# Gated linear attention into two MLPs: the attention's stack in aligned rows, its chunk ends by a small matmul, its small copies on another engine

## Chip, cores and metric

The kernel runs on one core of one Trainium2 chip. The metric is the device time of one launch in microseconds (us), the median of several runs. Engines are TensorE (PE; PEld is its weight load), VectorE (DVE), ScalarE (ACT), GpSimd (POOL) and SyncE (SP, which here issues all DMAs).

## Reference, cut to what matters

```python
batch, n_heads, seq, head_dim = (4, 8, 768, 48)
mag = np.sqrt(a_re * a_re + a_im * a_im)
scale = np.minimum(mag, 0.999) / (mag + 1e-06)
a_re_n, a_im_n = (a_re * scale, a_im * scale)
...
for t in range(S):
    new_re = ar * S_re - ai * S_im
    new_im = ar * S_im + ai * S_re
    kv = np.einsum('bhd,bhe->bhde', k[:, :, t], v[:, :, t])
    S_re, S_im = (new_re + kv, new_im)
    y[:, :, t] = np.einsum('bhd,bhde->bhe', q[:, :, t], S_re)
...
x = y.transpose(0, 2, 1, 3).reshape(3072, 384)
h = x @ w_in;  g = np.maximum(0.01 * h, h);  x = g @ w_out            # first MLP, d_ff 2048
h = x @ w_in2; g = np.where(h > 0, h, np.exp(np.minimum(h, 0)) - 1)   # second MLP, d_ff 2048
out = g @ w_out2
```

The weights come as 64-bit floats.

## The kernel before, in words

**Attention.** The sequence is cut into 6 chunks of 128 steps; a chunk of one batch entry is a tile, 24 in all (tile i is chunk i // 4 of batch entry i % 4). In a tile the 384 feature rows (8 heads of 48) lie on 128 partitions in 3 groups j, as [128, 3, 128]. The front half of `attention` (up to `yield`, L409 to L452) loads the decay's real and imaginary part, makes its magnitude with Ln and Exp on ScalarE, its running product by a scan on VectorE (L438), the ratio of imaginary to real part (L431) and clamps it (L432), copies the product at the chunk's end to `flags` on GpSimd (L446), and multiplies k and q by the product or its inverse (L452). The back half takes the arctangent, sums the phase by a scan (L462), takes off whole turns by adding and subtracting a large constant (L466, L467, both VectorE), carries the end's phase to the next chunk by a small GpSimd operation (L471), and writes k and q times cosine and sine into `st` (L481). `st` has 257 columns a row: 128 of k, 128 of q, and the chunk-end product, which GpSimd copies there (L479).

Features have to come from "group and partition" to "head by head, cosine over sine", so `st` goes to DRAM (L488) and returns as `f` (L491), 96 rows by 8 heads by 257. The scores of each head are one matmul (L520), masked on VectorE (L525). In tiles 0 to 2 (`EARLY`) the output is 8 matmuls (L535), a ScalarE copy (L539) and 3 transposes on PE (L545); in later tiles it is made transposed (L558, with the carried state L563), copied to `am` by ScalarE (L568), sent to DRAM by two DMAs (L572) and fetched back by one (L575). From either, `split` makes the 16-bit high part `xh` (ScalarE, L368) and the rest `xl` (VectorE, L369), the input of the first MLP. The state is updated by 8 matmuls (L591) and, in odd chunks, multiplied by the chunk-end product, the last column of `f` (L603).

**MLPs.** Tokens are worked in 8 blocks of 384 (3 tiles). All matmuls of the MLPs take 16-bit high and low parts, three products for each: per block and per 128 of d_ff, 9 matmuls into `h` (L620), then ScalarE and VectorE make g and split it into `gh` and `gl` (L628 to L636), then 9 matmuls into `acc` (L655). Blocks of the first and second MLP alternate after two of the first (`ORDER`). Weights are loaded (L325, L328), turned into 32-bit floats on VectorE (L346, L348, L351) and split (L357 ScalarE, L358 VectorE), 32 times. Checks of the inputs' range run on ScalarE (L337, L339, L375, L380, L386) wherever there is room.

**Order.** Nothing is scheduled by the chip or the compiler: `Plan` takes every operation with an estimated duration, its dependences and a due time, lists them by rank, repeats that `ROUNDS` times backwards and forwards, and keeps the best. The operations are then issued in that order, so each engine's queue is fixed, and one that waits holds up everything behind it. Where the plan leaves TensorE idle for more than 0.7 us, dummy matmuls on `ident` are put in (L773), one for each 0.22 us of the planned gap, so that its clock stays up.

## Time and profile before

| | |
|---|---|
| three runs | 978.29, 980.07, 984.93 us; median 980.07 |
| the profiled execution | 977.53 us, of which the span from first to last instruction is 975.7 us |
| TensorE's granted clock over the span | 0.978 of full speed |
| busy | PE 926.8, DVE 681.6, ACT 700.2, POOL 52.3 us |
| DMA | 129.15 MB, 132 GB/s over the span |

The profile is of one execution. A line such as L620 is a line of the kernel before. In a timeline row the two numbers are start and duration in us, and the bracket gives the idle time of the engine before it and what ended it. 32-bit matmuls show as two entries each. Consecutive instructions of one engine overlap a little, so the distance of their starts is what each takes from the engine.

### The profile page before, as it was taken

The numbers are of one execution on the slowest core, as the hardware profiler recorded it, in microseconds if no ns is written. First come the engines' busy times: TensorE is split into PE (matmuls) and PEld (weight loads), VectorE is DVE, ScalarE is ACT, GpSimd is POOL, SyncE is SP. The second block draws the span as 40 slices with busy tenths as digits, with TensorE's granted clock in tenths as the row PEclk, the third lists the DMA queues.
The fourth block names the chain that finished last, engine by engine and source line by source line (L and its number), as shares of the span: only waits on it lengthen the run. The fifth ranks groups of instructions, "written<-read, shape, count | busy, mean of one in ns | idle before, by whom it ended". The sixth has DMA issues, their size and how long they took to land.

```text
span 975.7 us, 17221 instructions
## 1 busy us (share of the span) xinstructions
PE 926.8 (95%) x6444; PEld 616.9 (63%) x6444; DVE 681.6 (70%) x1322; ACT 700.2 (72%) x1526; POOL 52.3 (5%) x113
## 2 busy tenths in 40 slices
PE   3488999999999999999999999999999999999997
PEld 3487666676755666666766667666666666666664
DVE  7998999999984685655786458637886444445452
ACT  6676669576998899999998456539798544345552
POOL 3103001010000000000010000000000000000000
PEclk8698999999999999999999999999999999999999
DMA  7797793776747836955846004405446021000000
GB/s 249 202 260 208 207 238 106 201 226 190 212 146 205 235 102 186 247 150 171 239 137 153 17 19 119 116 1 131 120 149 171 1 57 50 17 1 1 23 3 28
DMA packets 110028, 129.15 MB, mean 132 GB/s; under 512 B 6768, under 2 KB 98672, under 8 KB 109936
## 3 DMA queue, kind: packets, MB, share of 16 engines
q1 hardware_dynamic: 109936, 127.97, 47.9%
q8 instruction: 52, 0.85, 0.4%
q14 instruction: 40, 0.33, 0.1%
HBM read 100.15 MB, written 27.80 MB: 131 GB/s over the span
## 4 chain that ended last, share of the span: by engine, by line
PE 49%; ACT 20%; DVE 15%; DMA 10%; issue 4%; POOL 1%; SPq 0%; DVEq 0%; ACTq 0%; POOLq 0%
PE h L620 22%; PE acc L655 22%; ACT wr L339 5%; DMA stack_scratch<-st 4%; DMA wr<-in_w_in 3%; ACT wt L337 2%; ACT gh L368 2%; PE pa L520 2%; DMA re<-in_aa 2%; DVE g L633 2%; DVE wt L348 2%; DVE gl L369 2%; DVE wr L351 1%; DVE st L481 1%; ACT g L631 1%
## 5 line engine op out<-in xcount | busy, mean ns | idle before, releaser
L620 PEld LDWEIGHTS <-w 128*128 128x128 f16 x2304 | 225.5, 98 | 151.0 <-issue 8.0
L369 DVE TENSOR_TENSOR gl<-g,gh 128x384 f16<-128x384 f32 x256 | 141.8, 554 | 91.7 <-ACT gh L368 89.9
L655 PE MATMUL acc<-gh,w 128*128 128x384 f16 x768 | 187.3, 326 | 0.9 <-ACT gh L368 0.8
L368 ACT ACTIVATE gh<-g 128x384 f16<-128x384 f32 x256 | 132.6, 518 | 76.6 <-DVE g L633 73.6
L655 PE MATMUL acc<-w,gh 128*128 128x384 f16 x768 | 187.4, 326 | 0.0
L633 DVE SCALAR_TENSOR_TENSOR g<-h,g 128x384 f32<-128x384 f32 x256 | 141.6, 554 | 62.4 <-ACT g L628 59.1
L655 PEld LDWEIGHTS <-w 128*128 128x128 f16 x1152 | 112.6, 98 | 75.7 <-issue 2.5
L620 PE MATMUL h<-xh,w 128*128 128x384 f16 x768 | 146.6, 327 | 2.7 <-DVE g L633 2.7
L620 PE MATMUL h<-yh,w 128*128 128x384 f16 x768 | 146.8, 328 | 1.1 <-DVE g L633 1.1
L655 PE MATMUL acc<-gl,w 128*128 128x384 f16 x384 | 125.2, 326 | 0.2
L655 PE MATMUL acc<-w,gl 128*128 128x384 f16 x384 | 125.2, 326 | 0.1
L655 PEld LDWEIGHTS <-gh 128*128 128x128 f16 x768 | 74.5, 98 | 48.3 <-issue 0.9
L628 ACT ACTIVATE g<-h 128x384 f32<-128x384 f32 x128 | 61.8, 483 | 55.5 <-PE h L620 55.2
L630 ACT ACTIVATE g<-h 128x384 f32<-128x384 f32 x128 | 62.1, 485 | 48.2 <-PE h L620 45.9
L632 DVE TENSOR_SCALAR g<-g 128x384 f32<-128x384 f32 x128 | 45.6, 357 | 72.6 <-ACT g L631 72.4
L620 PE MATMUL h<-yl,w 128*128 128x384 f16 x384 | 83.4, 326 | 0.0
L620 PE MATMUL h<-xl,w 128*128 128x384 f16 x384 | 83.3, 326 | 0.0
L631 ACT ACTIVATE g<-g 128x384 f32<-128x384 f32 x128 | 66.1, 518 | 1.9
L339 ACT ACTIVATE wr<-wt,consts 128x768 f32<-128x768 f32 x64 | 64.1, 1002 | 0.4
L655 PEld LDWEIGHTS <-gl 128*128 128x128 f16 x384 | 37.6, 98 | 25.3 <-DVE gl L369 0.5
L520 PE MATMUL pa<-f 96*128 96x128 f32 x384 | 48.4, 276 | 4.4 <-DMA f<-stack_scratch 2.2
L520 PEld LDWEIGHTS pa<-f 96*128 96x128 f32 x384 | 46.6, 192 | 6.7 <-issue 3.2
(104 smaller groups left out, 1173.9 us busy)
## 6 DMA issues: line engine op xcount, KB each, us to landing
wr<-in_w_out SPq DMA_DIRECT2D x64, 384.0 KB, 3.9
wr<-in_w_in SPq DMA_DIRECT2D x64, 384.0 KB, 4.4
stack_scratch<-st SPq DMA_DIRECT2D x48, 385.5 KB, 5.0
f<-stack_scratch SPq DMA_DIRECT2D x48, 385.5 KB, 5.9
kq<-in_kq SPq DMA_DIRECT2D x24, 384.0 KB, 5.3
...
```

The lines of the kernel that those rows point to most:

```text
L337: plan.op("ACT", act(2 * DM), lambda: S_.activation(t.t, raw.t[:, :, :, 1].bitcast(F32), AF.Abs), r=both, w=[t])
L339: plan.op("ACT", act(2 * DM) + 2 * EXTRA, lambda side=side, scale=scale, bias=bias: S_.activation(raw.t[:, :, :, 0].bitcast(F32), t.t, AF. ...
L368: plan.op("ACT", eng, lambda: S_.activation(hi(), v(), AF.Copy), r=r, w=wh)
L369: plan.op("DVE", dve(n), lambda: V.tensor_tensor(lo(), v(), hi(), ALU.subtract), r=r + wh, w=wl)
L520: T_.matmul(pt.t[:, hh * C:(hh + 1) * C], lhsT=f.t[:, h, 0:C], rhs=f.t[:, h, C:2 * C], start=True, stop=True)
L620: T_.matmul(ph.t[:, :n], lhsT=w.t[:, 0, z, j * P:(j + 1) * P], rhs=x.t[:, j, :n], start=(m == 0), stop=(m == len(seq) - 1))
L628: plan.op("ACT", act(n, True), lambda: S_.activation(g.t[:, :n], ph.t[:, :n], AF.Copy, scale=0.01 * c), r=[ph], w=[g])
L630: plan.op("ACT", act(n, True), lambda: S_.activation(g.t[:, :n], ph.t[:, :n], AF.Relu, scale=-1.0 / (SX * SW)), r=[ph], w=[g])
L631: plan.op("ACT", act(n), lambda: S_.activation(g.t[:, :n], g.t[:, :n], AF.Exp, scale=-1.0), w=[g], table="L")
L632: plan.op("DVE", dve(n, True), lambda: V.tensor_scalar(g.t[:, :n], g.t[:, :n], -1.0, SG, ALU.add, ALU.mult), w=[g])
L633: plan.op("DVE", dve(n), lambda: V.scalar_tensor_tensor(g.t[:, :n], ph.t[:, :n], c, g.t[:, :n], ALU.mult, ALU.max), r=[ph], w=[g])
L655: T_.matmul(acc[o].t[:, :width], lhsT=pair[0], rhs=pair[1], start=(f == 0 and m == 0), stop=(f == KF - 1 and m == 2))
```

## The change

- Features are laid out another way: partition 16h + e, group j holds feature 3e + j of head h. So one partition's three rows of `st` are neighbours in DRAM, and a store is one run of 3072 bytes for each partition. The 257th column is gone: rows are 1024 bytes. The host lays out the inputs so; rows of `w_in` are permuted on the host (`X_ROWS`).
- The chunk-end product reaches the state by a matmul: in odd chunks VectorE spreads the three end values over 96 columns (`rows`), one matmul with a 0/1 matrix gives [96, 8] in PSUM, and the state is multiplied by that.
- The copies to `flags` and the carry run on VectorE; the two copies into `st` are gone. GpSimd has no work left in the loop.
- The clamp ahead of the arctangent is gone. The addition of the large constant to the phase runs on ScalarE.
- All tiles make the output transposed. `xh` and `xl` are made from PSUM directly; each has a fourth group that holds heads 6 and 7, and four small DMAs (16 partitions x 3 x 128 16-bit values, from `xh` into `xh` and from `xl` into `xl`) spread it over the partitions that the heads of 48 rows leave free. The DRAM round trip of the output and the transposes of the early tiles are gone.
- The plan's costs of the stack's DMAs are lower, its rounds 11 instead of 3. So the order of instructions is another one throughout.

```diff
-    ROUNDS = 3
+    ROUNDS = 11
...
+    nc.vector.tensor_reduce(row_of, ident.rearrange("p (h e) -> p e h", h=H), AX.X, ALU.add)
+    nc.vector.tensor_reduce(head_of, ident.rearrange("p (h e) -> p h e", h=H), AX.X, ALU.add)
...
-        plan.op("DVE", dve(N, True), lambda: V.tensor_scalar(w.t, w.t, -TAN_MAX * RC, TAN_MAX * RC, ALU.max, ALU.min),
-                w=[w])
...
-        plan.op("POOL", 200, lambda: G.tensor_copy(flags.t[:, 3:6, i], pr.t[:, :, 1, C - 1]), r=[pr], w=[f3])
+        plan.op("DVE", dve(KJ), lambda: V.tensor_copy(flags.t[:, 3:6, i], pr.t[:, :, 1, C - 1]), r=[pr], w=[f3])
...
-        plan.op("DVE", dve(N, True), lambda: V.tensor_scalar(nf.t, ph.t, MAGIC, None, ALU.add), r=[ph], w=[nf])
+        plan.op("ACT", act(N), lambda: S_.activation(nf.t, ph.t, AF.Copy, bias=MAGIC), r=[ph], w=[nf])
...
-            plan.op("POOL", 200, lambda: G.tensor_scalar(cr.t, nf.t[:, :, C - 1], -1.0, None, ALU.mult), r=[nf], w=[cr])
+            plan.op("DVE", dve(KJ), lambda: V.tensor_scalar(cr.t, nf.t[:, :, C - 1], -1.0, None, ALU.mult), r=[nf], w=[cr])
...
-        st = plan.buf(cp, [P, 2, KJ, CW], F32, "st", ST_BUFS)
+        st = plan.buf(cp, [P, 2, KJ, 2 * C], F32, "st", ST_BUFS)
-            plan.op("POOL", 200, lambda cs=cs: G.tensor_copy(st.t[:, cs, :, 2 * C], flags.t[:, 3:6, i]),
-                    r=[f3], w=[st.part(("e", cs))])
...
-            plan.op("SP", 1800, lambda cs=cs: nc.sync.dma_start(
-                scr[cs].rearrange("(j p) w -> p j w", p=P), st.t[:, cs]),
-                r=[st.part(("e", cs)), st.part(cs)], w=[dr.part(cs)])
-            plan.op("SP", 2350, lambda cs=cs: nc.sync.dma_start(
+            plan.op("SP", 1150, lambda cs=cs: nc.sync.dma_start(
+                scr[cs].rearrange("(p j) w -> p j w", j=KJ), st.t[:, cs]), r=[st.part(cs)], w=[dr.part(cs)])
+            plan.op("SP", 1900, lambda cs=cs: nc.sync.dma_start(
                 f.t[D * cs:D * (cs + 1)], scr[cs].rearrange("(h d) w -> d h w", d=D)), r=[dr.part(cs)], w=[f.part(cs)])
...
-                    kn.t[:, :, cs, :], pt.t[:, :DM].rearrange("p (h d) -> p h d", h=H), AF.Copy),
+                    kn.t[:, :, cs], pt.t[:, :DM].rearrange("p (j h e) -> p h e j", j=KJ, h=H), AF.Copy),
...
-        if i < EARLY:
...
-            plan.op("ACT", act(512, True), lambda: S_.activation(
-                yt.t[:wide].rearrange("p g t -> p (g t)"), py.t[:wide], AF.Copy, scale=SX), r=[py], w=[yt])
-            yd, ys = yt_dram[i % 2], plan.buf(None, None, None, "yscr", 2)
-            for r in range(2):
-                plan.op("SP", 290, lambda r=r: nc.sync.dma_start(
-                    yd.rearrange("(g r e) t -> r e g t", r=2, e=D)[r], yt.t[64 * r:64 * r + D]), r=[yt], w=[ys.part(r)])
-            y = plan.buf(cp, [P, KJ, C], F32, "y")
-            plan.op("SP", 1000, lambda: nc.sync.dma_start(y.t, yd.rearrange("(j p) t -> p j t", p=P)),
-                    r=[ys.part(0), ys.part(1)], w=[y])
...
-        split(lambda: xh.t[:, :, cut], lambda: xl.t[:, :, cut], xap, act(N, i < EARLY), N, [xsrc], [xh.part(q)],
-              [xl.part(q)])
+        py4 = lambda: py.t[:wide].rearrange("p (g t) -> p g t", g=4)
+        plan.op("ACT", act(512, True), lambda: S_.activation(xh.t[:wide, :, span], py4(), AF.Copy, scale=SX), r=[py], w=[xh])
+        plan.op("DVE", dve(512), lambda: V.scalar_tensor_tensor(
+            xl.t[:wide, :, span], py4(), SX, xh.t[:wide, :, span], ALU.mult, ALU.subtract), r=[py, xh], w=[xl])
+        for z, xz in enumerate((xh, xl)):
+            for r in range(2):
+                plan.op("SP", 200, lambda xz=xz, r=r: nc.sync.dma_start(
+                    xz.t[64 * r + D:64 * (r + 1), 0:KJ, span],
+                    xz.t[64 * r:64 * r + D, KJ, span]),
+                    r=[xz], w=[x1[k][z].part((q, r))])
...
             if c % 2:
-                plan.op("DVE", dve(N), lambda: V.tensor_tensor(state[b].t, state[b].t, pe(), ALU.mult),
-                        r=fp, w=[state[b]])
+                rows = plan.buf(cp, [P, 2, DE, KJ], F32, "rows")
+                plan.op("DVE", 120, lambda: V.tensor_tensor(
+                    rows.t, flags.t[:, 3:6, i].unsqueeze(1).unsqueeze(1).to_broadcast([P, 2, DE, KJ]),
+                    row_of.unsqueeze(1).unsqueeze(3).to_broadcast([P, 2, DE, KJ]), ALU.mult), r=[f3], w=[rows])
+                pe = pa()
+                plan.op("PE", 100, lambda: T_.matmul(
+                    pe.t[:2 * D, :H], lhsT=rows.t.rearrange("p a e j -> p (a e j)"), rhs=head_of, start=True, stop=True),
+                    r=[rows], w=[pe])
+                plan.op("DVE", dve(N), lambda: V.tensor_tensor(
+                    state[b].t, state[b].t, pe.t[:2 * D, :H].unsqueeze(2).to_broadcast([2 * D, H, D]), ALU.mult),
+                    r=[pe], w=[state[b]])
```

**Order on TensorE**, from the scores of tile 2 (L520 before, L510 in the change) to the first matmuls of the first MLP (L620, now L596). `pa` is a PSUM buffer of the attention, `h` the hidden layer's; L773, now L750, are the dummy matmuls. Before:

```order
L520 MATMUL pa<-f 128x128 x8
L773 MATMUL h<-ident 128x128 x6
L535 MATMUL pa<-v,am 128x48 x8
L773 MATMUL h<-ident 128x128 x2
L545 MATMUL pa<-ident,y 128x128 x3
L591 MATMUL pa<-v,kn 96x48 x8
L507 MATMUL pa<-ident,st 128x128 x3
L620 LDWEIGHTS w_143
L620 MATMUL h<-xh,w_143 128x384
```

In the change, the end of the same stretch (the output matmuls L530 come in four such pairs):

```order
L530 MATMUL pa<-am,v 64x128
L530 MATMUL pa<-am,v 48x128
L559 MATMUL pa<-v,kn 96x48 x8
L750 MATMUL h<-ident 128x128 x18
L596 LDWEIGHTS w_146
L596 MATMUL h<-xh,w_146 128x384
```

The transposes of y and those of tile 3's `st` are no longer ahead of the first MLP matmul; 18 dummy matmuls are.

**Order on VectorE** in the same stretch, from the first masking of tile 2 to its `xl`. `wt`, `wr` and `w` are a weight's stages, `t_` buffers are the attention's temporaries. Before:

```order
L525 TENSOR_TENSOR am<-pa,mask 128x512
L466 TENSOR_SCALAR t_765<-t_752 128x384
L525 TENSOR_TENSOR am<-pa,mask 128x512
L467 SCALAR_TENSOR_TENSOR t_765<-t_765,t_752 128x384
L346 TENSOR_SCALAR wt<-wr 128x768
L358 SCALAR_TENSOR_TENSOR w_750<-wr,w_750 128x2x384
L348 SCALAR_TENSOR_TENSOR wt<-wr,wt 128x768
L481 TENSOR_TENSOR st<-kq,t_790 128x3x256
L481 TENSOR_TENSOR st<-kq,t_765 128x3x256
L369 TENSOR_TENSOR xl<-pa,xh 128x3x128
```

In the change:

```order
L515 TENSOR_TENSOR am<-pa,mask 128x512
L432 SCALAR_TENSOR_TENSOR pr<-t_691,flags,consts 128x128 x3
L515 TENSOR_TENSOR am<-pa,mask 128x512
L347 TENSOR_SCALAR wt<-wr 128x768
L427 TENSOR_TENSOR t_736<-im,t_613 128x384
L349 SCALAR_TENSOR_TENSOR wt<-wr,wt 128x768
L440 COPY flags<-pr 128x3
L571 TENSOR_TENSOR rows<-flags,row_of 128x96
L352 SCALAR_TENSOR_TENSOR wr<-wr,wt 128x768
L544 SCALAR_TENSOR_TENSOR xl<-pa,xh 112x4x128
```

Tile 3's phase and its `st` stood between tile 2's masking and its `xl`; they have moved behind it, and work of a front half stands there.

**Order on SyncE's queue** from the stores of tile 0's stack to the loads of tile 1's. Before:

```order
L488 DMA stack_scratch<-st 128x3x257 x2
L451 DMA kq<-in_kq 128x768
L491 DMA f<-stack_scratch 48x8x257 x2
L328 DMA wr<-in_w_out 128x768
L325 DMA wr<-in_w_in 128x3x256
L488 DMA stack_scratch<-st 128x3x257 x2
L451 DMA kq<-in_kq 128x768
L328 DMA wr<-in_w_out 128x768
L325 DMA wr<-in_w_in 128x3x256
L491 DMA f<-stack_scratch 48x8x257
```

In the change:

```order
L480 DMA stack_scratch<-st 128x768 x2
L445 DMA kq<-in_kq 128x768
L482 DMA f<-stack_scratch 48x8x256 x2
L480 DMA stack_scratch<-st 128x768 x2
L445 DMA kq<-in_kq 128x768
L329 DMA wr<-in_w_out 128x768
L326 DMA wr<-in_w_in 128x3x256
L482 DMA f<-stack_scratch 48x8x256 x2
```

One pair of weight loads that stood ahead of tile 1's stores has moved away.

## Rows read from the trace of the kernel before

**Rows 1.** The page: PE and DVE busy in 40 slices (tenths).
```profile
PE   3488999999999999999999999999999999999997
DVE  7998999999984685655786458637886444445452
```

**Rows 2.** Stretches: length, busy PE, PEld, DVE, ACT, POOL; PE clock, DMA share, GB/s.
```profile
60.00:80.00 20.00, 17.79 (x160) 17.21 (x159) 19.01 (x38) 14.77 (x30) 4.56 (x4) 1.00 0.92 251
...
88.40:960.00 871.60, 862.14 (x5952) 557.37 (x5950) 600.87 (x1178) 638.72 (x1409) 31.63 (x74) 1.00 0.46 124
...
320.00:340.00 20.00, 18.09 (x137) 13.05 (x137) 13.40 (x28) 17.33 (x41) 1.25 (x4) 0.91 0.92 242
```

**Rows 3.** Timeline, 80 to 91 us, POOL, ACT, PE and DVE in turn.
```profile
80.51 3.08 POOL L471 TENSOR_SCALAR carry<-t 128x3 f32<-128x3 f32 x1 [2.77 <-DVE t L467]
...
83.62 0.52 ACT L476 ACTIVATE t<-t 128x384 f32<-128x384 f32 x1 [1.99 <-POOL carry L471]
...
84.57 0.90 PE L545 MATMUL pa<-ident,y 128*128 128x128 f32 x3 [2.84 <-ACT y L539]
85.27 2.69 PE L591 MATMUL pa<-v,kn 128*96 128x48 f32 x16
...
88.42 2.07 PE L620 MATMUL h<-xh,w 128*128 128x384 f16 x6
...
90.81 1.14 PE L620 MATMUL h<-xh,w 128*128 128x384 f16 x6
...
84.17 0.96 DVE L481 TENSOR_TENSOR st<-kq,t 128x768 f32<-128x768 f32 x1 [0.67 <-ACT t L476]
86.04 0.56 DVE L369 TENSOR_TENSOR xl<-pa,xh 128x384 f16<-128x384 f32 x1 [0.90 <-ACT xh L368]
```

**Rows 4.** Timeline of VectorE, 20 to 31 us.
```profile
20.81 0.55 DVE L448 TENSOR_TENSOR t<-pr,t 128x384 f32<-128x384 f32 x1
21.28 0.95 DVE L348 SCALAR_TENSOR_TENSOR wt<-wr,wt 128x768 int32<-128x768 int32 x1
22.15 0.55 DVE L449 SCALAR_TENSOR_TENSOR pr<-t,t 128x384 f32<-128x384 f32 x1
...
29.95 1.24 DVE L462 TENSOR_TENSOR_SCAN t<-t,consts 128x128 f32<-128x128 f32 x3
```

**Rows 5.** Groups: busy us, mean ns of one, idle before.
```profile
L525 DVE TENSOR_TENSOR am<-pa,mask 128x512 f32<-128x512 f32 x48 | 32.6, 683 | 7.3 <-PE pa L520 4.3 <-DMA turned_scratch<-am 3.1
...
L466 DVE TENSOR_SCALAR t<-t 128x384 f32<-128x384 f32 x24 | 8.5, 353 | 0.2
...
L746 DVE COPY ok<-subn 128x1 f32<-128x1 f32 x1 | 0.1, 146 | 0.0
...
L755 PE MATMUL pa<-consts,okr 128*1 128x1 f32 x2 | 0.2, 164 | 0.0
```

**Rows 6.** DMA issues: KB each, median us from issue to landing.
```profile
stack_scratch<-st SPq DMA_DIRECT2D x48, 385.5 KB, 5.0
f<-stack_scratch SPq DMA_DIRECT2D x48, 385.5 KB, 5.9
...
turned_scratch<-am SPq DMA_DIRECT2D x42, 96.0 KB, 2.6
```

**Rows 7.** Timeline of TensorE, 54 to 62 us.
```profile
54.77 1.48 PE L591 MATMUL pa<-v,kn 128*96 128x48 f32 x16
56.09 1.01 PE L507 MATMUL pa<-ident,st 128*128 128x128 f32 x6
56.93 4.85 PE L773 MATMUL h<-ident 128*128 128x128 f32 x42
```

**Rows 8.** The dummy matmuls alone (L773): stretch, PE and PEld busy, clock, DMA.
```profile
100.00:960.00 860.00, 4.43 (x28) 4.07 (x28) 1.00 0.45 123
```

**Rows 9.** Timeline of GpSimd, 11 to 25 us.
```profile
11.53 0.19 POOL L446 COPY flags<-pr 128x3 f32<-128x3 f32 x1 [9.35 <-DVE pr L438]
...
19.16 5.79 POOL L446 COPY flags<-pr 128x3 f32<-128x3 f32 x1 [5.93 <-DVE pr L438]
```

More of the change, by code (lines that the diff above doesn't have):

```diff
@@ L69 @@
 TWO_PI = 2.0 * math.pi * (1.0 - 2.0 ** -23)
-PIECES = []
-for _h in range(H):
-    _g = _h * D
-    while _g < (_h + 1) * D:
-        _e = min((_h + 1) * D, (_g // P + 1) * P)
-        PIECES.append((_h, _g - _h * D, _g % P, _g // P, _e - _g))
-        _g = _e
+DE = D // KJ
+X_ROWS = [[48 * (2 * j + p // 64) + p % 64 if p % 64 < 48 else 288 + 48 * (p // 64) + 3 * (p % 64 - 48) + j
+           for p in range(P)] for j in range(KJ)]
 def weight_f22(nc, pool, src, part, k, w):
@@ L500, in attention @@
         if not last:
-            kn = plan.buf(cp, [P, H, 2, D], F32, "kn", KN_BUFS)
+            kn = plan.buf(cp, [P, H, 2, DE, KJ], F32, "kn", KN_BUFS)
             for cs in range(2):
@@ L578, in attention @@
         k, q = place[i]
         if k not in x1:
-            x1[k] = [plan.buf(cp, [P, KJ, 384], F16, f"x{s}", X_BUFS) for s in "hl"]
-        xh, xl = x1[k]
-        cut = slice(q * P, (q + 1) * P)
-        split(lambda: xh.t[:, :, cut], lambda: xl.t[:, :, cut], xap, act(N, i < EARLY), N, [xsrc], [xh.part(q)],
-              [xl.part(q)])
-        squares([xh.part(q)], lambda: xh.t[:, :, cut], N, lambda: flags.t[:, 2, i:i + 1], flags.part((2, i)))
+            x1[k] = [plan.buf(cp, [P, KJ + 1, 384], F16, f"x{s}", X_BUFS) for s in "hl"]
@@ new lines, in attention, with ym @@
+        wide = D + 64
+        def ym():
+            for g in range(4):
+                for r in range(2):
+                    h = 2 * g + r
+                    cols = h * D, (h + 1) * D + (0 if r else 64 - D)
+                    T_.matmul(py.t[64 * r:64 * r + cols[1] - cols[0], g * C:(g + 1) * C],
+                              lhsT=v.t.rearrange("p h d -> p (h d)")[:, cols[0]:cols[1]], rhs=am[h // 4].t[:, h % 4, :],
+                              start=True, stop=(c == 0))
+                for r in range(2) if c else ():
+                    h = 2 * g + r
+                    T_.matmul(py.t[64 * r:64 * r + D, g * C:(g + 1) * C], lhsT=state[b].t[:, h, :],
+                              rhs=f.t[:, h, C:2 * C], start=False, stop=True)
@@ new lines, in attention @@
+        plan.op("PE", 8 * YNS * (2 if c else 1), ym, r=fp + [*am, v] + ([state[b]] if c else []), w=[py],
+                due=tile_due(i))
+        span = slice(q * P, (q + 1) * P)
+        xh, xl = (x.part(q) for x in x1[k])
+        py4 = lambda: py.t[:wide].rearrange("p (g t) -> p g t", g=4)
+        plan.op("ACT", act(512, True), lambda: S_.activation(xh.t[:wide, :, span], py4(), AF.Copy, scale=SX), r=[py], w=[xh])
+        plan.op("DVE", dve(512), lambda: V.scalar_tensor_tensor(
+            xl.t[:wide, :, span], py4(), SX, xh.t[:wide, :, span], ALU.mult, ALU.subtract), r=[py, xh], w=[xl])
@@ new lines, in attention @@
+        for z, xz in enumerate((xh, xl)):
+            for r in range(2):
+                plan.op("SP", 200, lambda xz=xz, r=r: nc.sync.dma_start(
+                    xz.t[64 * r + D:64 * (r + 1), 0:KJ, span],
+                    xz.t[64 * r:64 * r + D, KJ, span]),
+                    r=[xz], w=[x1[k][z].part((q, r))])
+        parts = [xh, x1[k][0].part((q, 0)), x1[k][0].part((q, 1))]
+        squares(parts, lambda: xh.t[:, 0:KJ, span], N, lambda: flags.t[:, 2, i:i + 1], flags.part((2, i)))
@@ L635, in hidden @@
         gh, gl = (plan.buf(cp, [P, 384], F16, f"g{z}", G_BUFS) for z in "hl")
-        split(lambda: gh.t[:, :n], lambda: gl.t[:, :n], lambda: g.t[:, :n], act(n), n, [g], [gh], [gl])
+        plan.op("ACT", act(n), lambda: S_.activation(gh.t[:, :n], g.t[:, :n], AF.Copy), r=[g], w=[gh])
+        plan.op("DVE", dve(n), lambda: V.tensor_tensor(gl.t[:, :n], g.t[:, :n], gh.t[:, :n], ALU.subtract), r=[g, gh], w=[gl])
         return gh, gl
```

89 lines of the change are left out of this document (28 added, 61 removed).

## Prediction

> **What bounds the kernel now.** First the slices of the page [rows 1]: TensorE is at 3 to 8 tenths in the first four slices (98 us) and at 9 from there to the end, while VectorE is full up to the tenth slice and about half idle from the twelfth on. So there are two stages with two limits. Next the stretches [rows 2]: from the first MLP matmul at 88.4 us to 960 us TensorE is busy 862.1 of 871.6 us, so this stage is TensorE's own work, with 9.5 us of waiting in it. In the head, VectorE is busy 19.0 of 20 us between 60 and 80 us, while TensorE spends its time on dummy matmuls.
>
> What ends the head is read from the timeline around 80 to 91 us [rows 3]. GpSimd's carry of three values a partition (L471) takes 3.08 us; ScalarE waits 1.99 us for it, with the copy of y (L539) behind it in its queue; TensorE waits 2.84 us for that copy, then transposes; `xl` of the third tile (L369) starts at 86.04 us, and the first MLP matmul (L620) at 88.42 us.
>
> The change can act in three places: the head, the 9.5 us of waits behind it, and TensorE's own work. It leaves the MLP's matmuls as they are.
>
> **The head.** VectorE is in order and nearly full, so I count what stands ahead of the third tile's `xl`. What an instruction takes is the distance of starts [rows 4]: 0.47 us for 384 columns (20.81 to 21.28), 0.87 us for 768 (21.28 to 22.15); three scans 1.24 us less the overlap of 0.08 to 0.1 us, about 1.1 us as a mean of the forms; masking 0.68 us less the overlap, 0.6 us [rows 5]; a fast 384-column operation 0.35 us less the overlap, 0.27 us [rows 5].
>
> Before, the order has there 47 operations of 384 columns (22.1 us), 41 of 768 (35.7), 10 groups of scans (11.0), 10 fast ones (2.7), 6 maskings (3.6) and a cast (0.2): 75.3 us. `xl` started at 86.04 us, so VectorE lost 10.7 us to waits. The last two waits, 0.67 and 0.90 us [rows 3], are those for GpSimd's carry, 1.6 us.
>
> In the change the same count is 40 of 384 columns (18.8), 37 of 768 (32.2), 9 groups of scans (9.9), 9 of 512 (maskings and `xl`, 5.4), 9 small copies, `rows`, a cast and two reductions (1.4 together): 67.7 us. Small copies I take at 0.08 us each: the row of a one-column copy has 0.146 us [rows 5], from which the overlap goes; at the full 0.146 us the nine cost 0.6 us more. Of the 7.6 us less, 2.7 are gone for good (clamps and additions); some 6.5 us (a weight, tile 3's phase and stack, a front half's end) are only moved behind the first MLP matmul; 1.6 us are new.
>
> With the other waits as they were, `xl` of the third tile starts at 67.7 + 10.7 - 1.6 = 76.8 us and ends at 77.4 us. Then two small DMAs must land, which before had no counterpart in the head. No row shows a DMA from on-chip memory to itself; the nearest is the store to `turned_scratch`, 2.6 us [rows 6], and with 0.5 us for the two issues the data is there at 80.5 us. Bounds: nothing, if TensorE is later anyway, and the 5.9 us of a whole stack load [rows 6].
>
> TensorE is later: its order ends with the 8 matmuls of the state's update (1.48 us) and 18 dummy matmuls; 21 of these took 4.85 us [rows 7], so 18 take 4.2 us. The output matmuls end with what `xh` reads, about 76.2 us; 76.2 + 1.5 + 4.2 = 81.9 us. I take 81.9 us for the first MLP matmul, 6.5 us earlier than before.
>
> TensorE's clock adds to this. Before, behind the 2.84 us wait, the 8 matmuls of the update took 2.69 us instead of 1.48 us [rows 3, 7], and the first six MLP matmuls 2.07 us, where the next six like them took 1.14 us. In the change dummy matmuls keep it busy, so another 0.9 us comes back. The head gives 7.4 us.
>
> Bounds: 2.0 us at least, ScalarE's wait for the carry, if all else turns up again; 10 us at most, if the stack's way through DRAM is shorter too. That way is 5.0 + 5.9 us [rows 6]; rows of 1024 bytes, runs of 3072 and one weight's pair of loads less ahead of it speak for shorter, and I count nothing for it, since VectorE, with less to do, will wait for it sooner: between tile 0's `st` and its masking there are 9 us of other work in the change, against 12 us before.
>
> On the GpSimd copies the trace first: the same copy to `flags` takes 0.19 us at 11.5 us and 5.79 us at 19.16 us [rows 9], in a stretch where VectorE runs one two-input operation after another [rows 4]. The Trainium skill (SBUF — State Buffer, section Who interferes with whom) says that a VectorE instruction with two on-chip inputs and a GpSimd instruction that reads that memory block each other for whole instructions. The rows agree with that. By the rule every such wait goes with the change; by the trace most of them held up nobody on the path, and only the one above is in the sum.
>
> **TensorE's work behind the head.** Added are 8 matmuls for the chunk ends, two passes each. A lone pass took 0.164 us [rows 5], so 0.33 us each or 2.6 us if they queue badly, and 0.19 us each if they follow as the update's passes do (1.48 us for 16) [rows 7]. I take 2.0 us. Three transposes of tile 3 move behind the first MLP matmul: half of 1.01 us [rows 7], 0.5 us. Together +2.5 us, bounds 1.5 to 5.
>
> **The waits behind the head.** There are 9.5 us [rows 2], and 28 entries of dummy matmuls, 4.4 us [rows 8], that were put in because the plan itself saw TensorE idle: 13.9 us. The change has two dummy matmuls behind the first MLP matmul and none later. It also takes latency off: no DRAM round trip for the output, `am` no longer waits for a DMA to read it (3.1 us of VectorE's waits at L525 [rows 5]), `f` is free sooner. But waits that the plan does not see (a late DMA, a queue on ScalarE) stay. I take half of the 13.9 us as gone, 6.9 us; bounds are a loss of 4 us and the whole.
>
> **What costs nothing, and its cover.** The 6.5 us moved on VectorE lie beside the first block's matmuls, and VectorE is idle for 871.6 - 600.9 = 271 us of the stage [rows 2]; if that cover is missing in the first 100 us, they come back. ScalarE gains an addition per tile (24 of 384 columns) and loses a pass over the output (it makes `xh` straight from PSUM): even. Its copy of `kn` reads PSUM across groups; no row shows such a read, I take no change, at twice 0.48 us it would be 19 us of ScalarE's 233 idle. SyncE's queue gets 4 small DMAs a tile for 3 larger ones.
>
> **The sum.** Against the profiled execution's own 977.5 us: -7.4 - 6.9 + 2.5 = -11.8, so 965.7 us. The median of the runs shown, 980.07, is 2.5 us above that execution; I forecast 968 us for a median, with 963 to 973 us as this case's own range.
>
> **Rivals.**
> 1. The head's gain is given back: VectorE's 6.5 us of moved work delay the first two blocks and the waits stay at 13.9 us. Then -7.4 + 2.5 and up to +6.5: 975 to 982 us. For it: VectorE is full in slices 6 to 10 [rows 1]. Against: TensorE is at 9 there too. Chance 0.27, taken at 977.
> 2. The output's PSUM buffer is held longer. Before, from tile 3 on, one ScalarE copy freed it; now VectorE's `xl` must have read it too, and TensorE, in order, stops with MLP matmuls behind the attention step that needs a buffer (three rotate). If VectorE has one 768-column and one 512-column operation ahead, that is 0.87 + 0.6 = 1.5 us a tile, 21 tiles, 31 us: 999 us. It makes the kernel slower by over 1% from 1.05 us a tile. Against: the masking holds such buffers for VectorE in the same way (48 times), and TensorE does not show it. Chance 0.08.
> 3. All goes well: the head gives 10 us, the waits vanish: 977.5 - 10 - 13.9 + 2.5 + 2.5 = 959 us. Chance 0.13.
> 4. The small DMAs are slow. The Trainium skill (DMA: Bandwidth & Descriptors, section Specifications) asks for pieces of 512 bytes or more for full rate, while its section Why small descriptors are slow (HBM only) exempts transfers inside the chip; the pieces here have 256. No row of before shows one. Were landing 5.9 us, the stack load's, instead of 2.6 us, the first MLP matmul would come at 83.8 us, 1.9 us later: 970 us. Chance 0.07.
>
> **How the numbers follow.** The forecast has 0.45. About 1% is what a measurement of this kernel can tell from no change, so the limits are 970.3 and 989.9 us. Faster: most of the forecast (0.37), rival 3 (0.13) and some of rival 4 (0.04), 0.54. Slower: rival 2, 0.08. Same: the rest, 0.38. The range 958 to 980 leaves out rival 2 and the ends of rivals 1 and 3.
>
> **What would show it right or wrong.** Right: the first MLP matmul between 79 and 84 us; GpSimd idle after the start; TensorE idle behind it for some 5 to 9 us; 8 short matmuls with 8 columns, about 0.2 us each. Wrong: a first MLP matmul after 86 us; TensorE waiting for VectorE's `xl` or a PSUM buffer of the attention; more idle TensorE behind the head than 14 us.

## The result, and the profile after

The changed kernel took 992.92 us (median of 4 runs, 991.79 to 997.44), the kernel before, on the same chip, 979.86 us: a ratio of 1.0126, 95% interval 1.0081 to 1.0171. It is slower by 1.3%; the forecast was 968 us, and the range up to 980 us does not hold it. The execution that was profiled has a span of 990.0 us, 14.3 us more than before.

The page's slices after, as [rows 1] and with the clock (TensorE, VectorE, granted TensorE clock):

```profile
PE   4498989999899899999989999999999999999997
DVE  7878989999786568755677558855587554445553
```

TensorE is no longer at 9 throughout from the fifth slice on: there are 8s up to the twenty-first. The stretches, as [rows 2] (length, busy PE, PEld, DVE, ACT, POOL; PE clock, DMA share, GB/s), one from the first MLP matmul to 960 us and one to the end:

```profile
60.00:80.00 20.00, 14.46 (x136) 13.42 (x136) 14.66 (x29) 10.85 (x23) 0.00 (x0) 0.94 0.68 191
89.60:960.00 870.40, 852.29 (x5859) 548.51 (x5857) 594.07 (x1173) 632.67 (x1397) 0.00 (x0) 0.99 0.40 117
...
89.60:990.00 900.40, 875.09 (x5999) 562.02 (x5996) 604.24 (x1194) 643.14 (x1417) 0.00 (x0) 0.99 0.39 114
```

The kernel before, to its end, and in a stretch that is needed below:

```profile
88.40:975.70 887.30, 870.68 (x6004) 562.33 (x6001) 603.77 (x1184) 641.45 (x1414) 31.63 (x74) 0.99 0.45 123
...
100.00:240.00 140.00, 138.02 (x1002) 92.03 (x1001) 137.79 (x245) 96.63 (x204) 11.80 (x15) 1.00 0.71 194
```

So the 14.3 us are: first MLP matmul 1.2 us later (89.6 against 88.4), TensorE busy 4.4 us more behind it (875.1 against 870.7), idle 8.7 us more (25.3 against 16.6). Up to 960 us, where the tail is left out, the idle time is 18.1 us against 9.5 us.

A part of the longer busy time is clock. Of the stretches of 20 us between 100 and 960 us, three have a granted clock below 1.00 in the change (0.97 from 240 to 260 us and the two below), and TensorE had waited 1.96 us up to 259.4 us and 2.57 us up to 502.5 us; before there is one (0.91, from 320 us, [rows 2]):

```profile
260.00:280.00 20.00, 20.00 (x140) 14.01 (x140) 15.88 (x31) 14.25 (x34) 0.00 (x0) 0.86 0.33 103
...
500.00:520.00 20.00, 17.46 (x133) 12.26 (x134) 14.16 (x30) 16.20 (x36) 0.00 (x0) 0.91 0.50 147
```

Where the head lost its gain is in the timeline of VectorE and TensorE (as [rows 3]):

```profile
65.69 0.93 DVE L349 SCALAR_TENSOR_TENSOR wt<-wr,wt 128x768 int32<-128x768 int32 x1
71.97 0.69 DVE L544 SCALAR_TENSOR_TENSOR xl<-pa,xh 112x512 f16<-112x512 f32 x1 [5.34 <-DMA xh<-xh]
...
83.84 0.69 DVE L544 SCALAR_TENSOR_TENSOR xl<-pa,xh 112x512 f16<-112x512 f32 x1 [1.41 <-DMA xh<-xh]
...
69.37 2.02 PE L510 MATMUL pa<-f 96*128 96x128 f32 x16 [0.25 <-DMA f<-stack_scratch]
71.23 1.95 PE L750 MATMUL h<-ident 128*128 128x128 f32 x16
77.86 1.12 PE L530 MATMUL pa<-am,v 128*64 128x128 f32 x8 [4.68 <-DVE am L515]
...
80.63 2.80 PE L559 MATMUL pa<-v,kn 128*96 128x48 f32 x16
83.22 6.53 PE L750 MATMUL h<-ident 128*128 128x128 f32 x36
89.59 1.14 PE L596 MATMUL h<-xh,w 128*128 128x384 f16 x6
```

VectorE stands still for 5.34 us at tile 1's `xl`, until a DMA from `xh` into `xh` has landed; the maskings of tile 2 (L515) are behind it in the queue, and TensorE waits 4.68 us for them. After this wait TensorE's granted clock falls to 0.50 of full speed, the lower of its two levels (1.2 of 2.4 GHz), in the stretch from 80 to 88 us, so the state's update (L559) and the dummy matmuls (L750) behind it take longer too. The queue of SyncE shows that this DMA was issued at 66.21 us, ahead of `xl`; it landed 5.7 us later:

```profile
66.21 0.59 SPq L548 DMA_DIRECT2D xh<-xh  x1
72.69 1.20 SPq L548 DMA_DIRECT2D xl<-xl  x2
```

Over the whole kernel the waits for it are (who for whom, us in total, times, longest):

```profile
DVE xl L544 <- DMA xh<-xh: 21.3, 9, 5.3
...
ACT o L382 <- DMA xh<-xh: 6.2, 7, 2.0
```

The reason is in the code. `xl` is made on partitions 0 to 111 in one instruction, and reads `xh` there. Partitions 48 to 63 of these are where one of the DMAs writes the spread rows of heads 6 and 7. What `xl` makes of them is written over by its own DMA, so no value is needed; but a DMA that is issued first has to be waited for. The plan was told only that the DMA reads `xh` (`r=[xz]`), and put it ahead of `xl` wherever that suited it.

DMA issues after, as [rows 6]: the stack's way is shorter mainly on the store's side (3.9 us against 5.0, the load 5.6 against 5.9), and the small DMAs land in 1.8 us as a median of all 48; at the longest it was 7.7 us.

```profile
stack_scratch<-st SPq DMA_DIRECT2D x48, 384.0 KB, 3.9
f<-stack_scratch SPq DMA_DIRECT2D x48, 384.0 KB, 5.6
...
xh<-xh SPq DMA_DIRECT2D x48, 12.0 KB, 1.8
xl<-xl SPq DMA_DIRECT2D x48, 12.0 KB, 1.8
```

### The profile page after: what moved, and what is told of

It reads as the page before. It is cut to its first block, busy times and chain, and to the rows that moved or that the text cites. A ratio compares the mean times of both kernels' runs of the same rounds, so it can differ in the third digit from the quotient of the medians.

```text
span 990.0 us, 17096 instructions
## 1 busy us (share of the span) xinstructions
PE 931.8 (94%) x6441; PEld 616.9 (62%) x6441; DVE 677.9 (68%) x1328; ACT 700.4 (71%) x1526; POOL 1.5 (0%) x21
## 4 chain that ended last, share of the span: by engine, by line
PE 52%; ACT 19%; DVE 16%; DMA 9%; issue 3%; SPq 1%; DVEq 0%; ACTq 0%
PE acc L632 22%; PE h L596 22%; ACT wr L340 3%; DMA wr<-in_w_in 3%; PE pa L510 2%; ACT gh L612 2%; DMA xh<-xh 2%; DMA f<-stack_scratch 2%; DVE st L473 2%; DVE w L359 2%; ACT wt L338 2%; PE h L750 2%; DVE wt L349 2%; DVE g L609 1%; DVE wr L352 1%
## 5 line engine op out<-in xcount | busy, mean ns | idle before, releaser
L596 PEld LDWEIGHTS <-w 128*128 128x128 f16 x2304 | 225.2, 98 | 151.7 <-issue 8.5
L612 ACT ACTIVATE gh<-g 128x384 f16<-128x384 f32 x256 | 133.2, 521 | 90.9 <-DVE g L609 88.4
L596 PE MATMUL h<-yh,w 128*128 128x384 f16 x768 | 146.5, 327 | 3.2 <-DVE g L609 3.2
L596 PE MATMUL h<-xh,w 128*128 128x384 f16 x768 | 145.7, 326 | 0.5 <-DVE g L609 0.2
L596 PE MATMUL h<-xl,w 128*128 128x384 f16 x384 | 83.3, 326 | 0.0
L596 PE MATMUL h<-yl,w 128*128 128x384 f16 x384 | 83.3, 326 | 0.0
L510 PE MATMUL pa<-f 96*128 96x128 f32 x384 | 49.7, 282 | 6.3 <-DMA f<-stack_scratch 3.4
L510 PEld LDWEIGHTS pa<-f 96*128 96x128 f32 x384 | 47.8, 197 | 9.2 <-issue 3.3
```

Of the source, the lines that this page charges most:

```text
L510: T_.matmul(pt.t[:, hh * C:(hh + 1) * C], lhsT=f.t[:, h, 0:C], rhs=f.t[:, h, C:2 * C], start=True, stop=True)
L596: T_.matmul(ph.t[:, :n], lhsT=w.t[:, 0, z, j * P:(j + 1) * P], rhs=x.t[:, j, :n], start=(m == 0), stop=(m == len(seq) - 1))
L612: plan.op("ACT", act(n), lambda: S_.activation(gh.t[:, :n], g.t[:, :n], AF.Copy), r=[g], w=[gh])
```

## The experiments

Each was timed beside the kernel before. In the table, "rounds" are the plan's `ROUNDS`, "first" is the start of the first MLP matmul and "idle" TensorE's idle time from there to 960 us, both in the profiled execution. "Known" means that the plan knows that the small DMAs come behind `xl`; "prices" are what the plan is told of the stack's store and load, in ns.

| run | kernel | ratio to before, 95% | first, us | idle, us |
|---|---|---|---|---|
| | before (prices 1800, 2350) | 1 | 88.4 | 9.5 |
| | the change (1150, 1900) | 1.0126 (1.0081 to 1.0171) | 89.6 | 18.1 |
| e1 | the change, DMAs issued behind xl | 1.0008 (0.9978 to 1.0038) | 81.7 | 18.2 |
| e2 | the change, known | 1.0003 (0.9979 to 1.0026) | 81.8 | 15.2 |
| e3 | the change, 3 rounds | 1.0153 (1.0120 to 1.0186) | 88.5 | 23.0 |
| e4 | before, 11 rounds | 1.0064 (1.0041 to 1.0087) | 90.3 | 18.0 |
| e5 | known, prices 2200, 3900 | 1.0058 (1.0028 to 1.0089) | 109.8 | 5.1 |
| e6 | known, 3 rounds | 0.9966 (0.9942 to 0.9991) | 81.1 | 13.3 |
| e7 | before with the small edits | 0.9965 (0.9934 to 0.9996) | 86.7 | 15.7 |
| e8 | known, GpSimd's copies back | 0.9970 (0.9943 to 0.9997) | 79.2 | 14.0 |
| e9 | known, start put off | 1.0061 (1.0031 to 1.0092) | 91.0 | 15.3 |
| e10 | known, maskings twice | 1.0071 (1.0040 to 1.0102) | 81.0 | 23.1 |
| e11 | known, copies back, 3 rounds | 1.0028 (0.9997 to 1.0058) | 79.9 | 17.2 |
| e12 | known, without the small edits | 0.9958 (0.9925 to 0.9991) | 80.4 | 11.3 |
| e13 | known, old prices | 0.9858 (0.9824 to 0.9891) | 87.8 | 7.5 |
| e14 | known, old prices, 3 rounds | 0.9870 (0.9829 to 0.9911) | 87.1 | 7.1 |
| e15 | before, new prices | 1.0259 (1.0206 to 1.0311) | 82.2 | 30.3 |
| e16 | known, prices 1500, 2800 | 0.9895 (0.9864 to 0.9927) | 88.5 | 9.1 |
| e17 | the change, old prices | 1.0057 (1.0035 to 1.0080) | 92.3 | 13.2 |
| e18 | e12 with old prices | 0.9882 (0.9845 to 0.9919) | 90.5 | 8.8 |

**The wait of xl (e1, e2).** First only the place of the DMAs' issue, with the order of PE, VectorE and ScalarE as in the change:

```diff
+    held, done, queue = {}, set(), []
     for n in order:
+        if n in late and late[n] not in done:
+            held.setdefault(late[n], []).append(n)
+            continue
+        done.add(n)
+        queue.append(n)
+        queue.extend(held.pop(n, []))
+    order = queue
```

> The changed kernel, with each small DMA that spreads xh issued behind the VectorE operation that makes xl of the same tile; the order on PE, VectorE and ScalarE stays what it was, on SyncE's queue six of these DMAs move back by a few places. Theory A (VectorE's xl waits for the DMA of xh, because that DMA writes partitions which xl's read of xh covers, and so stalls VectorE and all behind it): VectorE's wait for that DMA falls from 21.3 us to nothing, the first MLP matmul comes at 82 to 84 us instead of 89.6 us, and the time falls by 8 to 13 us, to 980 to 985 us. Rival B (the other order of instructions is what costs, wherever its waits are): the wait goes, the head gains, but the first MLP matmul's 6 us are all, 985 to 988 us. Rival C (VectorE is late anyway): no change beyond 2 us.

Then the plan is told of it, and makes another order:

```diff
-                    r=[xz], w=[x1[k][z].part((q, r))])
+                    r=[xz, xl], w=[x1[k][z].part((q, r))])
```

> The changed kernel, where the plan itself is told that the DMAs of xh must not start before xl is made, so that the whole order is made anew. Theory A: as with the DMAs moved by hand, 976 to 985 us, since the plan now places work where VectorE would have stood. Rival B (orders of this planner scatter by more than the wait is worth): anything from 975 to 995 us, unlike the run with the order kept.

Medians of 982.77 and 979.41 us. The end of the head in e1, the first MLP matmul of e2, and what `xl` waits for in e2:

```profile
76.25 1.56 PE L563 MATMUL pa<-v,kn 128*96 128x48 f32 x16
77.65 4.25 PE L754 MATMUL h<-ident 128*128 128x128 f32 x36
81.73 1.14 PE L600 MATMUL h<-xh,w 128*128 128x384 f16 x6
```

```profile
81.84 1.14 PE L596 MATMUL h<-xh,w 128*128 128x384 f16 x6
...
DVE xl L544 <- ACT xh L543: 6.3, 8, 1.7
```

`xl`'s waits for the DMA are gone, the first MLP matmul comes 7.8 us sooner than in the change, and the kernel is as fast as before. So the waits of `xl` are the loss of 1.2%, and it is those in the head that cost: behind the start the idle time is the same in e1 as in the change (18.2 and 18.1 us). Some 3.5 of the 7.8 us come from the lower clock behind the wait: the update and the 36 passes of dummy matmuls took 2.80 and 6.53 us in the change and take 1.56 and 4.25 us in e1. But the head is now 6.6 us shorter than before, as forecast, and the end is not earlier: against before, e2 has 6.6 us less in the head, 2.8 us more busy TensorE and 5.7 us more idle.

**Rounds of planning (e3, e4, e6).** `ROUNDS` 11 to 3 in the change, 3 to 11 in the kernel before, 11 to 3 in e2.

> The changed kernel with 3 rounds of planning, as before the change. Theory A: ten of the xl operations still wait for a DMA, 988 to 997 us. Rival B (the order that eleven rounds pick is the bad one): 985 us or less.

> The kernel before, with 11 rounds of planning. Theory A: within 6 us of before, 974 to 986 us. Rival B (eleven rounds overfit the plan's own times): 988 us or more.

> As the run in which the plan knows of xl, with 3 rounds of planning instead of 11. It shows how far two orders of the same instructions lie apart. If orders scatter by several us (as the two pairs with other rounds so far, +4 and +8 us): 979 to 988 us with the first MLP matmul still at 81 to 84 us and the difference in TensorE's waits behind it. If the order hardly matters once the wait for the DMA is known to the plan: 977 to 982 us.

Going to 3 rounds adds 0.3% in the change and takes 0.4% off e2, going to 11 adds 0.6% before: the rounds are not the cause. e4's 987.9 us lies between the ranges of its two theories. Two orders of the same instructions, made with the same prices, lie 0.1 to 0.6% apart (e8 against e11 and e13 against e14 also); smaller differences between re-planned kernels are not read as an edit's worth.

**The small edits and GpSimd (e7, e8, e11, e12).** e7 is the kernel before with three of the edits, e8 is e2 with two of them taken back:

```diff
-        plan.op("DVE", dve(N, True), lambda: V.tensor_scalar(w.t, w.t, -TAN_MAX * RC, ...
-        plan.op("DVE", dve(N, True), lambda: V.tensor_scalar(nf.t, ph.t, MAGIC, None, ALU.add), ...
+        plan.op("ACT", act(N), lambda: S_.activation(nf.t, ph.t, AF.Copy, bias=MAGIC), ...
-        plan.op("POOL", 200, lambda: G.tensor_copy(...   (and the carry, and the two copies into st)
+        plan.op("DVE", dve(KJ), lambda: V.tensor_copy(...
```

> The kernel before with the small edits alone: the arctangent's clamp gone, the phase's rounding begun on ScalarE, and all small copies (flags, carry, stack ends) on VectorE; the stack, the chunk ends and the output's way through DRAM as before. Theory A (the small edits carry the head's gain): GpSimd's waits are gone (1.99 us on ScalarE, 1.6 us on VectorE) and VectorE has 2.7 us less to do, so the first MLP matmul comes at 84 to 86 us instead of 88.4, and if nothing is given back the time is 974 to 977 us. Theory B (what the head gains is given back in the stage behind it): the first MLP matmul is as early as that, but the time is 978 to 984 us.

> As the run in which the plan knows of xl, with the flags' copy and the carry back on GpSimd. If the copies matter as in the kernel before (GpSimd's 3 to 6 us beside VectorE's two-input operations): the first MLP matmul 1.6 to 4 us later, at 83.5 to 86 us, and the time 979 to 984 us. If the end is set by what the stage behind the head can take in: the first MLP matmul is as late as that, but the time stays at 978 to 981 us.

> As the run with the plan knowing of xl and the flags' copy and the carry on GpSimd, with 3 rounds of planning. The two runs that each had one of these were 0.3% faster than before. If both gains are properties of the edits they add up: 970 to 975 us. If they are two draws from a scatter of orders some 5 us wide: 976 to 984 us.

> The aligned rows, the small matmul for the chunk ends and the output's way without DRAM, with the plan knowing of xl, and none of the small edits: the clamp is there, the phase's rounding is begun on VectorE, and the flags' copy and the carry are on GpSimd. The small edits alone took 0.35% off the kernel before. If the two parts add up to the whole mended change: 979 to 984 us, and the first MLP matmul 1.5 to 3 us later than with the edits (79.2 us with the copies on GpSimd), at 81 to 82 us. If the aligned part alone carries what there is: 975 to 979 us.

e7 starts the MLP 1.8 us sooner (86.7 us, where 84 to 86 was expected) and ends within the scatter of orders. In e8 GpSimd's copies take as long as before, as its timeline and waits show, and yet the first MLP matmul is 2.6 us sooner than in e2, not later:

```profile
12.06 0.19 POOL L440 COPY flags<-pr 128x3 f32<-128x3 f32 x1 [9.88 <-DVE pr L432]
19.90 5.79 POOL L440 COPY flags<-pr 128x3 f32<-128x3 f32 x1 [7.65 <-DVE pr L432]
...
ACT t L470 <- POOL carry L465: 2.1, 2, 1.5
```

Nobody waits for the copy to `flags`, and ScalarE 2.1 us in all for the carry. Both theories of that run fall: in this order TensorE does not stand behind GpSimd. As e8's order is a new one, it does not measure what the carry cost in the kernel before. The gains of e6 and e8 do not add up in e11 (1.0028): two draws. e12 (0.9958) fits the theory that the aligned part alone carries what there is.

**Is an earlier start paid back as such? (e9, e10).** Both keep e2's order on every engine. e9 adds 28 dummy matmuls ahead of the first MLP matmul, e10 repeats each masking from the fourth tile on:

```diff
+    first = next(n for n in order if n in mlp)
+    idle[first] = idle.get(first, 0) + 28
```

```diff
-            plan.op("DVE", dve(512), lambda m=m, pt=pt: V.tensor_tensor(... ALU.mult), r=[pt], w=[m])
+            plan.op("DVE", dve(512), lambda m=m, pt=pt: [V.tensor_tensor(... ALU.mult)
+                for _ in range(2 if i > 2 else 1)], r=[pt], w=[m])
```

> As the run in which the plan knows of xl, with every engine's order as there and 28 more dummy matmuls ahead of the first MLP matmul, some 6.6 us (40 passes took 4.70 us there), so that it starts at about 88.4 us, as in the kernel before. Theory A (the head's gain is paid back behind it: an earlier start only means waiting later for VectorE's work and the stack): TensorE's idle time behind the start falls by 4 us or more from 22.3 us, and the time is within 2.5 us of 979.4 us. Theory B (the waits behind the head are the order's own and have nothing to do with the start): they stay, and the time is 984 to 987 us.

> As the run in which the plan knows of xl, with every engine's order as there, but from the fourth tile on VectorE does each masking of the scores twice (the same values again): 0.6 us more, 8 times between 82 and 250 us, 42 times in all. Theory A (VectorE, 94% busy from 100 to 240 us, sets how fast TensorE is fed there): the first MLP matmul stays at 82 us and the time grows by 4 to 7 us, to 983 to 986 us. Theory B (VectorE's idle 8 us there cover it; what TensorE waits for is the stack's way through DRAM or SyncE's queue): the time grows by 2 us or less, to at most 981.5 us.

The stretches of e2, e9 and e10 from the first MLP matmul to 960 us:

```profile
81.84:960.00 878.16, 863.00 (x5935) 556.62 (x5936) 603.05 (x1190) 639.01 (x1412) 0.00 (x0) 0.99 0.40 116
```

```profile
90.97:960.00 869.03, 853.71 (x5886) 551.55 (x5884) 595.42 (x1174) 633.42 (x1401) 0.00 (x0) 1.00 0.40 117
```

```profile
81.02:960.00 878.98, 855.88 (x5885) 549.80 (x5886) 624.45 (x1222) 635.43 (x1405) 0.00 (x0) 1.00 0.40 116
...
PE h L596 <- DVE g L609: 6.5, 8, 2.3
PE pa L497 <- DVE xl L544: 2.9, 2, 2.4
PE pa L530 <- DVE am L515: 2.8, 4, 1.6
```

Theory A of e9 falls: the start came 9.1 us later (2.5 more than meant), the end 7.8 us, and the idle time stayed at 15.3 us. In a given order an earlier start is real. In e10, VectorE's extra 0.73 us for each masking made the idle time 7.9 us longer and the span 8.1 us, 1 us more than its theory A allowed, with TensorE standing behind VectorE's `g`, `xl` and `am`. So VectorE has no slack that would take in more work; which of its work stands where is what the order decides.

**The prices of the stack (e5, e13 to e16).** The change lowers two numbers of the plan, which the forecast never priced. e13 is e2 with the old numbers put back:

```diff
-            plan.op("SP", 1150, lambda cs=cs: nc.sync.dma_start(
+            plan.op("SP", 1800, lambda cs=cs: nc.sync.dma_start(
...
-            plan.op("SP", 1900, lambda cs=cs: nc.sync.dma_start(
+            plan.op("SP", 2350, lambda cs=cs: nc.sync.dma_start(
```

> As the run in which the plan knows of xl, but the plan is told a longer stay of the stack: 2200 ns for the store and 3900 ns for the load instead of 1150 and 1900, near the 3.8 and 5.7 us that they took from issue to landing there. Theory A (the head's gain is given back because the plan puts the scores of tiles 3 to 6 where it believes f to be, and TensorE, in order, stands there until f lands): TensorE's idle time from the first MLP matmul to the end falls from 22.3 us to 12 to 17 us, no wait over 1 us for f between 100 and 290 us, time 970 to 975 us. Theory B (the data cannot be there sooner, whatever the plan believes; the waits only change their name, or come back as dummy matmuls): 977 to 984 us, and idle time plus dummies stays at 20 us or more.

> As the run in which the plan knows of xl, but with the prices that the kernel before gave the stack's two DMAs (1800 and 2350 ns in place of 1150 and 1900). Theory P (the plan places the scores too early because it believes f sooner than it lands): TensorE's idle time from the first MLP matmul to 960 us falls from 15.2 us to 8 to 11 us with the first MLP matmul still at 81 to 85 us; 970 to 975 us. Theory S (each plan is another draw, the price does not rule): idle between 11 and 18 us, 975 to 986 us.

> As the run with the old prices, with 3 rounds of planning. Theory P: as that run, idle 8 to 11 us, 970 to 975 us. Theory S: another draw, 975 to 986 us, not on the same side as the run with 11 rounds in idle time.

> The kernel before, unchanged but for the plan's prices of the stack's two DMAs, which are the change's (1150 and 1900 ns in place of 1800 and 2350). Theory P: TensorE's idle time from the first MLP matmul to 960 us rises from 9.5 us to 13 to 18 us, with waits for f; 984 to 990 us. Theory S: 976 to 988 us, with idle time on either side of 9.5 us.

> As the run in which the plan knows of xl, with 1500 and 2800 ns for the stack's two DMAs, which took 3.8 and 5.7 us from issue to landing there. Theory P: idle between the run with the old prices and the 4.6 us of the run with 2200 and 3900 ns, 6 to 10 us, and 968 to 974 us if the MLP starts before 85 us. Theory S: 975 to 986 us, idle between 11 and 18 us.

e13 took 969.68 us where before took 983.72, e14 969.45; e15, which alters nothing of the kernel before but two numbers of the plan, 1007.78 us. First e13, then e15: the start, the stretch to 960 us, and for e15 TensorE's longest waits and the DMA's landing:

```profile
86.77 0.84 PE L497 MATMUL pa<-ident,st 128*128 128x128 f32 x6 [0.52 <-DVE st L473]
87.77 1.14 PE L596 MATMUL h<-xh,w 128*128 128x384 f16 x6 [0.15 <-ACT t L467]
...
87.77:960.00 872.23, 864.77 (x5985) 558.67 (x5985) 598.80 (x1183) 637.28 (x1408) 0.00 (x0) 1.00 0.39 116
...
100.00:240.00 140.00, 140.00 (x1000) 93.30 (x998) 139.34 (x252) 101.35 (x215) 0.00 (x0) 1.00 0.63 190
```

```profile
82.21 1.14 PE L620 MATMUL h<-xh,w 128*128 128x384 f16 x6
...
82.21:960.00 877.79, 847.46 (x5795) 545.06 (x5795) 598.00 (x1167) 627.83 (x1390) 29.76 (x76) 0.99 0.46 126
...
PE h L620 <- DVE g L633: 9.8, 13, 2.1
PE pa L520 <- DMA f<-stack_scratch: 9.5, 6, 2.8
PE acc L655 <- ACT gh L368: 4.4, 4, 2.1
...
93.86 1.82 DVE L481 TENSOR_TENSOR st<-kq,t 128x768 f32<-128x768 f32 x2
...
f<-stack_scratch SPq DMA_DIRECT2D x48, 385.5 KB, 5.8
```

With the new prices the kernel before starts the MLP at 82.2 us too: tile 3's `st`, which stood at 84.17 us ahead of tile 2's `xl` [rows 3], comes at 93.86 us behind it. But `f` lands in 5.8 us whatever the plan believes (5.9 in [rows 6]), TensorE then waits 9.5 us for it and for everything that was put behind it, and the idle time is 30.3 us, about twice what theory P expected, with a time far above its 990 us. With the old prices the change makes tile 3's stack first (the transposes at 86.77 us), starts at 87.8 us, and from 100 to 240 us TensorE is not idle at all. Too long a price is no good either: in e5 the idle time falls to 5.1 us, but the MLP starts at 109.8 us, which neither of its theories had.

What the prices do shows in the scores, which read `f`: TensorE's idle time ahead of them behind 90 us, in the kernel before, in e2 and in e13 (what ended it is inferred):

```profile
L520 PE MATMUL pa<-f 96*128 96x128 f32 x336 | 42.4, 275 | 2.4 <-DMA f<-stack_scratch 2.0 <-issue 0.4
...
L510 PE MATMUL pa<-f 96*128 96x128 f32 x336 | 44.0, 285 | 8.3 <-DMA xh<-xh 2.9 <-ACT t L422 2.1 <-DMA f<-stack_scratch 1.7
...
L510 PE MATMUL pa<-f 96*128 96x128 f32 x336 | 42.4, 275 | 0.0
```

Theory P holds for idle time and time (e13 and e14 come out a little below its ranges, e16 inside them), not for the start, which comes at 87 to 88.5 us in these three. That they are not draws is shown by five pairs that differ in the prices alone (before and e15, the change and e17, e2 and e13, e6 and e14, e12 and e18): the old prices are faster in each, by 0.7 to 2.6% of the time.

**Both together, and the parts at equal prices (e17, e18).**

> The change as given, with nothing altered but the two prices of the stack's DMAs (1800 and 2350 ns, as before). If the two faults add up, each with what it cost beside the other (the wait of xl 13.5 us, the prices 10 to 13 us): 980 to 985 us, ratio 0.996 to 1.0, xl still waiting for the DMA that spreads xh, 8 or more times and some 20 us in all. If the short prices are what lets that wait hurt (with more room in the plan nobody stands behind it): 970 to 976 us with the same waits on VectorE.

> The aligned rows, the matmul for the chunk ends and the output's way without DRAM alone (clamp there, rounding begun on VectorE, flags' copy and carry on GpSimd), with the plan knowing of xl and the old prices. At equal prices the small edits alone gave 0.9965 and the whole mended change 0.9858. If the parts add up: 0.987 to 0.992, 971 to 976 us. If the small edits are worth nothing beside the aligned rows: 0.983 to 0.987, 967 to 971 us.

The four corners: the change 1.0126, known 1.0003, old prices 1.0057, both 0.9858. Of the 2.7% between the first and the last, knowing alone mends 1.2 and the prices alone 0.7; together they mend 0.8 more than that sum, which is little beyond the scatter of orders. In e17, just above the 980 to 985 us expected of two faults that add up, VectorE still waits for the DMA:

```profile
DVE xl L544 <- DMA xh<-xh: 19.3, 7, 5.0
```

At old prices the aligned rows, with the way of the output and of the chunk ends, give 0.9882, with the small edits 0.9858; the small edits alone 0.9965. The difference of the small edits is within the scatter of orders, so what they are worth is open; the aligned part's 1.2% is not, though it stands on one plan.

## Why the prediction was wrong

**The step that failed first** is, as it stood, "With the other waits as they were, `xl` of the third tile starts at 76.8 us". It started at 83.84 us, 7.0 us later, since the change makes a wait that was not there: `xl` behind the DMA into `xh`, 5.34 and 1.41 us in the head. In e1, without it, this `xl` starts at 77.91 us. I looked at the DMA as something that comes after `xl` and must land before the first MLP matmul, because the plan's dependences say so; the waits of the instruction itself, which come from the partitions that it reads, were not read. By e1, with the order on the other engines in place, it is worth 1.2% of the time. The clock made it dearer: 18 dummy matmuls were taken at 4.2 us and the update at 1.48 us, and behind the wait they took 6.53 and 2.80 us.

Rival 4 priced the landing of the third tile's small DMAs, and there the 2.6 us taken were nearer than 5.9 us: they landed in 1.8 us in the change and in 1.8 to 2.2 us in e1. But the second tile's DMA that `xl` waited for took the 5.7 us of that rival. A stack load, a load of `v` and two weight loads were issued in the 2.1 us before it; no run shows which of them made it late. The Trainium skill (DMA: Bandwidth & Descriptors, section Why small descriptors are slow (HBM only)) exempts transfers inside the chip from the penalty on small pieces; the 1.8 us of these 256-byte pieces agree with it, and no run here varies the size of a piece.

**The head.** Without that wait it came at 81.73 and 81.84 us, where 81.9 was forecast; 18 or 20 dummy matmuls and the state's update end it as counted. The 0.9 us of clock came too: the first six MLP matmuls take 1.14 us in the change, e1 and e2, where they took 2.07 us. But the reason was not seen: by e15, which starts at 82.2 us without any of the edits, and e13, which has the edits and starts at 87.8 us, the 6.5 us are the work that the new prices move behind the start, not what the edits take off.

**"What costs nothing, and its cover"** is the second step that failed: "VectorE is idle for 871.6 - 600.9 = 271 us of the stage". That is an average over a stage in two parts: from 100 to 240 us VectorE is busy 137.8 of 140 us before, and the prediction's own first paragraph had read it as full up to the tenth slice (244 us). e10 shows what work put there costs. The text had said that the 6.5 us come back if the cover is missing, and rival 1 gave this 0.27 and 975 to 982 us; once the wait of `xl` is gone (e2: 979.4 us), this rival is what happened in time and place: from 100 to 240 us TensorE is idle 7.6 us in e2, against 2.0 us before.

```profile
100.00:240.00 140.00, 132.42 (x934) 87.25 (x932) 131.65 (x240) 95.44 (x203) 0.00 (x0) 0.99 0.61 179
```

The way there was only in part the rival's: 3.2 of these 7.6 us are waits for VectorE's `g` and `gl`, 3.7 lie ahead of the scores. e13, with the same instructions in another order, has no idle TensorE there.

**The waits behind the head**, -6.9 us: in the change, idle time and dummies are 18.1 + 0.9 us instead of 13.9. In e13 they are 7.5 us with no dummies, so 6.4 us less, almost as forecast. Each of the two large terms came true in size, the head's with the new prices and the waits' with the old ones, but the sum took both from one plan. Against before, e13's 8.5 us are 0.6 of the head, 4.4 of dummies, 2.3 of idle time to the end and 1.1 of other TensorE work. So it is luck that e13's 969.7 us lie beside the forecast of 968 us: the head, counted at 7.4 us, gives 0.6.

**TensorE's added work**, +2.5 us with bounds of 1.5 to 5: the chunk ends took 2.2 us (16 passes of 0.209 us that overlap), where 2.0 was taken. But without dummies TensorE's busy time behind the start is 8.0 us longer in the change (874.2 against 866.3 us). The clock is part of it: 0.97, 0.86 and 0.91 over 20 us each are some 5.2 us of work at full speed that was lost, an estimate, against 1.8 us before. In e13, where no stretch of 20 us from 100 us on is below 1.00, this time is 1.1 us shorter than before.

**GpSimd's carry**: the 1.6 us of VectorE's waits for it were counted as gone. In e8, with the copies on GpSimd, the start was earlier than in e2, so in the new order the term does not show; what it was worth in the old order stays open, since e7, which starts 1.8 us sooner, has other edits beside it. The 5.79 us above fell again in a stretch where VectorE runs one two-input operation after another, and again nobody waited. The rule of the Trainium skill (SBUF — State Buffer, section Who interferes with whom) agrees with that row.

**Rival 2**, a PSUM buffer held by `xl`, shows once, for 2.0 us, in the change's waits of L510. The signs named for a wrong forecast (a start after 86 us, TensorE waiting for `xl` or a PSUM buffer, more than 14 us idle) all came.

Open is how far the best prices lie from those tried: 1500 and 2800 ns gave 0.9895, 1800 and 2350 gave 0.9858, which is the fastest version found and beats both kernels.
